# Second MoE of a fused FFT and MoE kernel: order of the products in its sums, and place of the next tile's x

## The chip, the cores and the metric

The kernel runs on one core of one Trainium2 chip. A time is the device time of one execution in microseconds (us); the figure for the kernel before is the median of three runs. Beside it stands one profiled execution, whose records the rows below come from. Its span is the time from its first to its last instruction.

## The reference

A real array x (8 x 3072 x 256) goes through two Fourier transforms, of which the real part is kept; the 24576 rows of 256 go through a first MoE layer (256 to 2048 and back), and then each row goes to one of eight experts:

```python
X = np.fft.fft(np.fft.fft(x, axis=1), axis=2).real
h = x @ w_in;  x = (h * np.clip(h + 3, 0, 6) / 6) @ w_out       # first MoE
logits = x @ w_gate                                            # second MoE, x is 24576 x 256
expert_idx = np.argmax(logits, axis=1)
gate_w = softmax(logits)[arange, expert_idx]
for e in range(8):
    xe = x[expert_idx == e]
    out[expert_idx == e] = gate_w * (np.maximum(xe @ w1[e], 0) @ w2[e])   # 256 -> 1024 -> 256
```

## The kernel before

The first 2085 us are the transforms and the first MoE, whose rows are scattered into one list per expert in HBM (`xs_dram`). The change is in what follows, the second MoE. It works through the lists in tiles of 512 rows (big) or 256 rows (small), each tile of one expert. Tiles 0 and 1 are big and belong to the fullest expert; then two or three big tiles and a small one take turns. 59 tiles run: 41 big and 18 small; the small ones are tiles 4, 7, 10, 13, 16, 20, 23 and so on up to tile 58, the last. Three more small tiles stand behind a condition at the end.

Numbers are kept as sums of two parts, a high one (rounded to the format of TensorE's products) and a low one (what the rounding left). A product of two numbers is three products of parts: high by high, high by low and low by high. For one tile (`tile_of`, L1106) this is done:

- `first` (L993), the w1 phase: eight groups of 128 inner columns, f = 0 to 7. Each group is a sum of six products (two halves k of the 256 input columns by the three of PASS, L259) into one bank of PSUM, `hp`; there are four such banks. ACT evicts the high part with the relu (L999, into `WA`), DVE makes the low part from the bank and the high part (L1000, into `WB`), and only then is the bank free.
- `second` (L1092), the w2 phase: for each 128 rows of the tile (four groups in a big tile, two in a small one) a sum of 24 products, f = 0 to 7 by the three of PASS, into a bank `op`. DVE scales it by the gate (L1100, `yo`) and POOL scatters the rows to the output (L149).
- `prep_w` (L875) splits the next tile's weights, which SP has loaded, into parts, in four pieces, two of w1 and two of w2. ACT rounds the high part (L882), and the low part is a subtraction (L189) on POOL, or on DVE for the first piece that is prepared in a small tile. There are two sets of weights: `TB`, `W2a` and `SC` with the raw loads `w1a`, `w2a`, `w2d`, and `W1b`, `W2b` with `w1b`, `w2b`; tiles take them in turn.
- `prep_x` (L887) does the same for the next tile's x. The transposing loads bring 16-bit halves; ACT copies one (L894) and DVE the other (L895) into `xf`; ACT rounds the high part (L896, `xT0`), DVE subtracts for the low part (L189, `xT1`); a cast (L900) or two small instructions (L903, L904) make the rows' addresses `dst`. There are two sets here too: `xa`, `xfa`, `xTa` and `xb`, `xfb`, `xTb`.

The code is written tile by tile (w1 of tile i, preparation for i + 1, loads for i + 2, w2 of tile i), but a scheduler sets the order in which each engine gets its instructions: it moves a preparation ahead as far as its buffers allow. On each engine the instructions then run in that order, each one waiting for what it needs. A preparation of weights stands in ACT's queue as soon as the old ones have their last reader, around the last w1 group of a tile.

Of the kernel before, what the change touches and what calls it, by code (L numbers as in the profile page):

```python
# [22 lines left out]
P = 128  # L23
NB, SEQ, D, DFF, NE, FF = 8, 3072, 256, 2048, 8, 1024
# [5 lines left out]
TBIG, TS = 512, 256  # L30
# [4 lines left out]
NEARLY = 2  # L35
# [39 lines left out]
def tile_fft_moe(ctx, tc, xr, xf, xcoef, w_in, w_out, w_gate, w1, w2, tabs, fm, misc, tri, sgn8, dstc, maskc, out):  # L75
# [70 lines left out]
    dve, act, pool, pe, sp = nc.vector, nc.scalar, nc.gpsimd, nc.tensor, nc.sync  # L146

    def scat(group, **kw):
        i = pool.indirect_dma_start(oob_is_err=False, **kw)  # L149
        tc.declare_no_dep(i.ins, group=group, reason="distinct rows")  # L150
        tc.add_to_no_dep_group(group, i.ins)
# [11 lines left out]
    def matmul(*a, **kw):  # L163
        i = pe.matmul(*a, **kw)  # L164
        if hold.get("steps"):
            tc.keep_in_program_order(i)

    def mm_group(dst, terms):
        for n, (l, r) in enumerate(terms):
            matmul(dst, l, r, start=(n == 0), stop=(n == len(terms) - 1))  # L170

    def pinned(i):
        if hold.get("fold"):
            tc.keep_in_program_order(i)
# [13 lines left out]
    def sub(eng, o, a, b):  # L188
        i = eng.tensor_tensor(out=o, in0=a, in1=b, op=ALU.subtract)  # L189
        pinned(i)  # L190
        return i
# [67 lines left out]
    PASS = ((0, 0), (0, 1), (1, 0))  # L259
# [354 lines left out]
    if True:  # L614
# [215 lines left out]
        hh = [[W.rearrange("p (f n) -> p f n", n=TBIG) for W in Ws] for Ws in (WA, WB)]  # L830
# [9 lines left out]
        def rows(i):  # L840
            return TBIG if order[i] < NBIG else TS

        def xset(i):
            return xsets[i if i < NEARLY else 2 * (i % 2)]

        def kset(i):
            return ksets[0 if i < NEARLY else (i - NEARLY + 1) % 2]
# [4 lines left out]
        def load_x(i):  # L852
            t = T[i] = {}
            n = rows(i)
            o = order[i] - NEARLY
            v = er[0:1, i:i + 1] if i < NEARLY else regs[0:1, 0, o:o + 1]
            r = ds(reg(v, NE * CAPR - n), n)
            t["gd"] = pk.tile([P, 4, 2], F32, tag="gd", name=f"gd{i}")[:, 0:n // P]
            sp.dma_start(t["gd"], xs.bitcast(F32)[r, D:D + 2].rearrange("(t p) c -> p t c", p=P))
            for w in range(2):  # L860
                for k in range(2):
                    c = w * D + k * P
                    sp.dma_start(xset(i)["x"][:, w, k, 0:n], xs16[r, c:c + P], transpose=True)

        def load_w(i):
            s = kset(i)
            o = order[i] - NEARLY
            e = reg(er[0:1, 2:3] if i < NEARLY else regs[0:1, 1, o:o + 1], NE - 1)
            sp.dma_start(s["w1"], w1[ds(e, 1)].rearrange("e (k p) f -> p (e k) f", p=P))
            for f0, f1, t in s["w2"]:  # L870
                sp.dma_start(t.rearrange("p (f d) -> p f d", d=D),
                             w2[ds(e, 1), f0 * P:f1 * P].rearrange("e (k p) d -> p (e k) d", p=P))


        def prep_w(i, eng):  # L875
            s = kset(i)
            pairs = [[t[:, k] for t in s["W1"]] + [s["w1"][:, k]] for k in range(2)]
            pairs += [[t[:, f0:f1] for t in s["W2"]] + [t.rearrange("p (f d) -> p f d", d=D)]
                      for f0, f1, t in s["w2"]]

            def go(n, hi, lo, raw):
                pinned(act.activation(hi, raw, AF.Copy))  # L882
                sub(eng(n), lo, raw, hi)

            return [lambda n=n, p=p: go(n, *p) for n, p in enumerate(pairs)]

        def prep_x(i):  # L887
            t, v = T[i], xset(i)
            n = rows(i)
            nt = n // P  # L890
            xf, t["xT"] = v["xf"][:, :, 0:n], [z[:, :, 0:n] for z in v["xT"]]
            h = xf.bitcast(U16).rearrange("p k (n w) -> p k n w", w=2)
            keep = tc.keep_in_program_order
            keep(act.activation(h[:, :, :, 1], v["x"][:, 0, :, 0:n], AF.Copy))  # L894
            keep(dve.tensor_copy(h[:, :, :, 0], v["x"][:, 1, :, 0:n]))  # L895
            act.activation(t["xT"][0], xf, AF.Copy)  # L896
            sub(dve, t["xT"][1], xf, t["xT"][0])
            t["dst"] = pk.tile([P, 4], I32, tag="dst", name=f"dst{i}")[:, 0:nt]
            if order[i] < NBIG:
                keep(dve.tensor_copy(t["dst"], t["gd"][:, :, 1]))  # L900
            else:
                inv = pk.tile([P, 2], F32, tag="inv", name=f"inv{i}")
                keep(dve.tensor_scalar(inv, iot, vld[:, order[i] - NBIG:order[i] - NBIG + 1], BIG, op0=ALU.is_lt, op1=ALU.mult))  # L903
                keep(dve.tensor_tensor(out=t["dst"], in0=inv, in1=t["gd"][:, :, 1], op=ALU.add))  # L904
# [20 lines left out]
        def plan_early():  # L925
            e0 = 8 * (NCH - EC) + 18 + RKW - 3
            fill[e0].append(lambda: None)
            pfill[e0].append(early_mm)
            fill[e0].append(early_pick)
            fill[e0 + 4].append(lambda: (first_sets(), load_x(0), load_w(0), load_x(1)))  # L930
            for n in range(4):
                fill[e0 + 6 + EG * n].append(lambda n=n: in_order(prep_w(0, lambda n: dve)[n]))
            fill[e0 + 10 + EX].append(lambda: prep_x(0))
# [59 lines left out]
        def first(i, then=None):  # L993
            s, xT, n = kset(i), T[i]["xT"], rows(i)
            for f in range(8):
                hi, lo = (h[f // 4][:, f % 4, 0:n] for h in hh)
                ps = h_ps.tile([P, 512], F32, tag="hp", name=f"hp{i}_{f}")[:, 0:n]
                mm_group(ps, [(s["W1"][a][:, k, f * P:(f + 1) * P], xT[c][:, k]) for k in range(2) for a, c in PASS])
                act.activation(hi, ps, AF.Relu)  # L999
                dve.scalar_tensor_tensor(out=lo, in0=ps, scalar=0.0, in1=hi, op0=ALU.max, op1=ALU.subtract)  # L1000
                if f == FL and then:
                    then()

        def rest():
# [5 lines left out]
            assert not (fill or pfill or mfill or afill)  # L1010

        first(0, rest)
        second_set()
        prep_x(1)


# [36 lines left out]
        def pick(r, v, o, sh):  # L1053
# [35 lines left out]
                          W1=[pt(f"W1b{n}", [P, 2, FF]) for n in range(2)], W2=[pt(f"W2b{n}", [P, 8, D]) for n in range(2)]))  # L1089
        xsets.append(dict(x=pt("xb", [P, 2, 2, TBIG], U16), xf=pt("xfb", [P, 2, TBIG], F32), xT=[pt(f"xTb{n}", [P, 2, TBIG]) for n in range(2)]))  # L1090

        def second(i):  # L1092
            s, t = kset(i), T.pop(i)
            nt = rows(i) // P
            yo = pd.tile([P, 4, D], F32, tag="yo", bufs=2, name=f"yo{i}")
            for j in range(nt):
                ps = o_ps.tile([P, 512], F32, tag="op", name=f"op{i}_{j}")
                mm_group(ps[:, 0:D], [(hh[a][f // 4][:, f % 4, j * P:(j + 1) * P], s["W2"][c][:, f]) for f in range(8)
                                      for a, c in PASS])
                dve.tensor_scalar(yo[:, j], ps[:, 0:D], t["gd"][:, j, 0:1], None, op0=ALU.mult)  # L1100
                scat("out", out=out, out_offset=IndirectOffsetOnAxis(ap=t["dst"][:, j:j + 1], axis=0),
                     in_=yo[:, j], in_offset=None, bounds_check=NTOK - 1)
# [3 lines left out]
        def tile_of(i):  # L1106
            if i:
                first(i)
            if i + 1 < last and i:
                if i + 1 >= NEARLY:  # L1110
                    for f in prep_w(i + 1, lambda n: pool if n or rows(i) == TBIG else dve):
                        f()
                prep_x(i + 1)
            if i and i + 2 < last:
                load_x(i + 2)
                load_w(i + 2)
            second(i)
# [5 lines left out]
        for i in range(last):  # L1123
            tile_of(i)
        n = nc.values_load(nus[0:1, 0:1], min_val=0, max_val=NSMALL, skip_runtime_bounds_check_because=why)
        with tc.If(n > NSMALL - SPARE):
            i0, last = last, full
            for i in range(i0, min(i0 + 2, full)):
                load_x(i)
                load_w(i)  # L1130
            for f in prep_w(i0, lambda n: pool):
                f()
            prep_x(i0)
            for i in range(i0, last):
                tile_of(i)
# [149 lines left out]
```

## Time and profile before

| | |
|---|---|
| median of the runs | 3274.42 us (3268.84 to 3277.36, three runs) |
| the profiled execution's own time | 3273.91 us |
| its span | 3272.1 us |
| mean granted clock of TensorE | 0.985 |
| second MoE: first product, tile 0 | 2088 us after the span's start |
| second MoE: last product, tile 58 | 3260 us |

The span is shared out by engines: TensorE's products (PE), its weight loads (PEld), VectorE (DVE), ScalarE (ACT), GpSimd (POOL) and SyncE's DMA queue (SP). A product is issued while the one before it is still running, so starts tell more than durations. The idle time that a row names is the time just before an instruction, with the instruction that ended it.

### The profile page before, as it was taken

What the parts mean: (1) busy time and instruction counts of PE and PEld (TensorE: products, weight loads), DVE (VectorE), ACT (ScalarE), POOL (GpSimd) and SP (SyncE); (2) the same over time, 40 slices, a digit from 0 to 9 for tenths busy, and PEclk for the clock granted to TensorE, in tenths of its full rate; (3) what the DMA queues carried; (4) which work ended last, traced back from release to release, by engine and by line L of the source; (5) the groups of instructions that cost most, each with busy time, mean ns of one, the idle gap of its engine ahead of it and who ended that gap; (6) DMA issues with size and microseconds to landing.
All of it is one profiled execution on the core that took longest, in us unless ns stands there. A gap on an engine that the chain in (4) does not pass through costs nothing.

```text
span 3272.1 us, 61901 instructions
## 1 busy us (share of the span) xinstructions
PE 3116.5 (95%) x23482; PEld 2983.7 (91%) x23482; DVE 2117.7 (65%) x3699; ACT 1952.4 (60%) x3339; POOL 2123.1 (65%) x1784
## 2 busy tenths in 40 slices
PE   5899999999999999999999999999999999999998
PEld 5889999999999999999999999988888888888887
DVE  8586777777777777777777666755555555555553
ACT  3566666666666666667666766654444454444453
POOL 5466766766766766766766665676666566666664
PEclk8899999999999999999999999999999999999999
DMA  5100100100100100100100002274555455555550
GB/s 184 62 27 16 44 24 16 43 24 16 44 24 16 44 24 16 44 24 16 34 14 16 15 14 53 63 200 149 147 154 152 140 166 152 149 147 155 145 173 26
DMA packets 256189, 243.14 MB, mean 74 GB/s; under 512 B 157739, under 2 KB 219020, under 8 KB 255888
## 3 DMA queue, kind: packets, MB, share of 16 engines
q1 hardware_dynamic: 234640, 184.66, 20.0%
q0 software_dynamic: 21248, 54.48, 4.6%
q8 instruction: 187, 3.06, 0.4%
q14 instruction: 114, 0.93, 0.1%
HBM read 159.71 MB, written 54.04 MB: 65 GB/s over the span
## 4 chain that ended last, share of the span: by engine, by line
PE 61%; DVE 22%; ACT 10%; issue 3%; POOL 2%; DMA 1%; SPq 0%; ACTq 0%; DVEq 0%; POOLq 0%
PE op L164 16%; PE acc L164 16%; PE hp L164 15%; PE ab L164 11%; DVE r L515 6%; ACT r L508 5%; DVE ab L186 3%; DVE ab L189 3%; ACT xp L546 1%; ACT gh L962 1%; DVE H L194 1%; ACT xo L539 1%; PE wi L164 1%; DVE H L186 1%; DVE xTa L189 1%
## 5 line engine op out<-in xcount | busy, mean ns | idle before, releaser
L189 POOL TENSOR_TENSOR gl<-r,gh 128x512 fp32r<-128x512 f32 x768 | 1018.7, 1349 | 541.4 <-ACT gh L962 536.7
L164 PE MATMUL acc<-WO,gh 128*128 128x264 f32 x6144 | 831.7, 286 | 4.5 <-ACT xo L539 2.3
L515 DVE SCALAR_TENSOR_TENSOR r<-r,ab 128x512 f32<-128x512 f32 x768 | 493.0, 683 | 460.8 <-ACT r L508 452.9
L164 PEld LDWEIGHTS acc<-WO,gh 128*128 128x128 f32 x6144 | 780.9, 190 | 6.5 <-ACT WO L182 3.3
L508 ACT ACTIVATE r<-ab,half 128x512 f32<-128x512 f32 x768 | 486.2, 684 | 241.0 <-DVE ab L186 219.5
L962 ACT ACTIVATE gh<-r 128x512 fp32r<-128x512 f32 x768 | 454.5, 628 | 203.2 <-PE acc L164 145.6
L1000 DVE SCALAR_TENSOR_TENSOR WB<-hp,WA 128x512 fp32r<-128x512 f32 (+1 forms) x472 | 278.7, 607 | 299.4 <-ACT WA L999 293.8
L164 PE MATMUL ab<-pq,WA 128*128 128x256 f32 x2304 | 398.3, 289 | 69.4 <-DVE r L515 63.6
L164 PE MATMUL acc<-WO,gl 128*128 128x264 f32 x3072 | 439.9, 285 | 0.0
L164 PEld LDWEIGHTS ab<-pq,WA 128*128 128x128 f32 x2304 | 330.6, 192 | 90.0 <-issue 82.4
L164 PEld LDWEIGHTS acc<-WO,gl 128*128 128x128 f32 x3072 | 402.8, 189 | 0.0
L999 ACT ACTIVATE WA<-hp 128x512 fp32r<-128x512 f32 (+1 forms) x472 | 241.4, 531 | 194.8 <-PE hp L164 192.7
L164 PE MATMUL ab<-pq,WB 128*128 128x256 f32 x2304 | 342.3, 285 | 0.0
L502 ACT ACTIVATE A<-ab 128x512 f32<-128x512 f32 x384 | 230.1, 599 | 158.7 <-PE ab L164 138.6
L149 POOL DMA_INDIRECT out_dram<-yo,dst x200 | 217.6, 1088 | 156.5 <-DVE yo L1100 119.4
L164 PEld LDWEIGHTS ab<-pq,WB 128*128 128x128 f32 x2304 | 307.7, 193 | 0.0
L164 PE MATMUL hp<-xTb,TB 128*128 128x512 f32 (+1 forms) x1344 | 277.3, 364 | 13.7 <-DVE WB L1000 13.5
L189 DVE TENSOR_TENSOR ab<-A,ab 128x512 f32<-128x512 f32 x384 | 264.7, 689 | 32.8 <-ACT A L502 25.3
L164 PEld LDWEIGHTS hp<-xTb,TB 128*128 128x128 f32 x1344 | 225.8, 188 | 57.9 <-DVE WB L1000 15.2
L164 PE MATMUL hp<-xTa,W1b 128*128 128x512 f32 (+1 forms) x1392 | 275.6, 357 | 1.6 <-DVE WB L1000 1.6
L164 PE MATMUL op<-W2b,WA 128*128 128x256 f32 x1536 | 275.0, 281 | 0.0
L186 DVE TENSOR_TENSOR ab<-A,ab 128x512 f32<-128x512 f32 x384 | 266.8, 695 | 11.5
(269 smaller groups left out, 5300.8 us busy)
## 6 DMA issues: line engine op xcount, KB each, us to landing
w1a<-in_w_dram SPq DMA_DIRECT2D x29, 1024.0 KB
w1b<-in_w_dram SPq DMA_DIRECT2D x29, 1024.0 KB
w2b<-in_w_dram SPq DMA_DIRECT2D x58, 512.0 KB
R<-in_xr_dram SPq DMA_DIRECT2D x32, 774.0 KB
w2a<-in_w_dram SPq DMA_DIRECT2D x29, 768.0 KB
w2d<-in_w_dram SPq DMA_DIRECT2D x28, 256.0 KB
q<-pq SPq DMA_DIRECT2D x288, 1.0 KB
raw<-in_w_in_dram SPq DMA_DIRECT2D x8, 512.0 KB
```

The lines of the kernel that those rows point to most:

```text
L149: i = pool.indirect_dma_start(oob_is_err=False, **kw)
L164: i = pe.matmul(*a, **kw)
L186: pinned(eng.tensor_tensor(out=o, in0=a, in1=b, op=ALU.add))
L189: i = eng.tensor_tensor(out=o, in0=a, in1=b, op=ALU.subtract)
L194: pinned(dve.scalar_tensor_tensor(out=o, in0=a, scalar=s, in1=b, op0=ALU.mult, op1=ALU.add))
L502: act.activation(A, h[0], AF.Copy)
L508: act.activation(r, h, AF.Relu, bias=half, scale=1.0 / 6.0)
L515: dve.scalar_tensor_tensor(out=g, in0=r, scalar=1.0, in1=h, op0=ALU.min, op1=ALU.mult)
L539: act.activation(xo[:, t, :], acc[t][:, 0:GW], AF.Copy)
L962: act.activation(gh[n], r[n], AF.Copy)
L999: act.activation(hi, ps, AF.Relu)
L1000: dve.scalar_tensor_tensor(out=lo, in0=ps, scalar=0.0, in1=hi, op0=ALU.max, op1=ALU.subtract)
```

## The change

Three things. In the w1 sums all products with the high part of x come first and those with its low part last. In the w2 sums all products with the high parts of the inner rows come first, f = 0 to 7, and those with the low parts last. `prep_x` of the next tile is called between the two w1 pieces and the two w2 pieces of `prep_w` instead of behind all four, and its subtraction is done in two halves.

```diff
--- before.py
+++ after.py
@@ -894,7 +894,8 @@
             keep(act.activation(h[:, :, :, 1], v["x"][:, 0, :, 0:n], AF.Copy))
             keep(dve.tensor_copy(h[:, :, :, 0], v["x"][:, 1, :, 0:n]))
             act.activation(t["xT"][0], xf, AF.Copy)
-            sub(dve, t["xT"][1], xf, t["xT"][0])
+            for k in range(2):
+                sub(dve, t["xT"][1][:, k], xf[:, k], t["xT"][0][:, k])
             t["dst"] = pk.tile([P, 4], I32, tag="dst", name=f"dst{i}")[:, 0:nt]
             if order[i] < NBIG:
                 keep(dve.tensor_copy(t["dst"], t["gd"][:, :, 1]))
@@ -995,7 +996,7 @@
             for f in range(8):
                 hi, lo = (h[f // 4][:, f % 4, 0:n] for h in hh)
                 ps = h_ps.tile([P, 512], F32, tag="hp", name=f"hp{i}_{f}")[:, 0:n]
-                mm_group(ps, [(s["W1"][a][:, k, f * P:(f + 1) * P], xT[c][:, k]) for k in range(2) for a, c in PASS])
+                mm_group(ps, [(s["W1"][a][:, k, f * P:(f + 1) * P], xT[c][:, k]) for c in range(2) for k in range(2) for a in range(2 - c)])
                 act.activation(hi, ps, AF.Relu)
                 dve.scalar_tensor_tensor(out=lo, in0=ps, scalar=0.0, in1=hi, op0=ALU.max, op1=ALU.subtract)
                 if f == FL and then:
@@ -1095,8 +1096,8 @@
             yo = pd.tile([P, 4, D], F32, tag="yo", bufs=2, name=f"yo{i}")
             for j in range(nt):
                 ps = o_ps.tile([P, 512], F32, tag="op", name=f"op{i}_{j}")
-                mm_group(ps[:, 0:D], [(hh[a][f // 4][:, f % 4, j * P:(j + 1) * P], s["W2"][c][:, f]) for f in range(8)
-                                      for a, c in PASS])
+                mm_group(ps[:, 0:D], [(hh[a][f // 4][:, f % 4, j * P:(j + 1) * P], s["W2"][c][:, f])
+                                      for a in range(2) for f in range(8) for c in range(2 - a)])
                 dve.tensor_scalar(yo[:, j], ps[:, 0:D], t["gd"][:, j, 0:1], None, op0=ALU.mult)
                 scat("out", out=out, out_offset=IndirectOffsetOnAxis(ap=t["dst"][:, j:j + 1], axis=0),
                      in_=yo[:, j], in_offset=None, bounds_check=NTOK - 1)
@@ -1107,10 +1108,9 @@
             if i:
                 first(i)
             if i + 1 < last and i:
-                if i + 1 >= NEARLY:
-                    for f in prep_w(i + 1, lambda n: pool if n or rows(i) == TBIG else dve):
-                        f()
-                prep_x(i + 1)
+                w = prep_w(i + 1, lambda n: pool if n or rows(i) == TBIG else dve) if i + 1 >= NEARLY else []
+                for f in w[:2] + [lambda: prep_x(i + 1)] + w[2:]:
+                    f()
             if i and i + 2 < last:
                 load_x(i + 2)
                 load_w(i + 2)
```

What this makes of the order is shown at three places. In these rows WA is the high and WB the low part of the inner rows (0 for f = 0 to 3, 1 for f = 4 to 7), xT0 and xT1 are the high and low part of x, W2a and SC those of w2; the names carry the tile and the group (hp7_6 is group 6 of tile 7) and a buffer number.

The first place is TensorE in small tile 7, at the end of its w1 phase. Before:

```order
L164 MATMUL op7_0_29120<-W2a0_26224,WA0_69 128x256
L164 MATMUL op7_0_29120<-SC1_74,WA0_69 128x256
L164 MATMUL op7_0_29120<-W2a0_26224,WB0_71 128x256
L164 MATMUL op7_0_29120<-W2a0_26224,WA0_69 128x256
L164 MATMUL hp7_7_29081<-xTb0_27630,TB_73 128x256
L164 MATMUL hp7_7_29081<-xTb1_27631,TB_73 128x256
L164 MATMUL hp7_7_29081<-xTb0_27630,TB_73 128x256 x2
L164 MATMUL hp7_7_29081<-xTb1_27631,TB_73 128x256
L164 MATMUL hp7_7_29081<-xTb0_27630,TB_73 128x256
L164 MATMUL op7_0_29120<-SC1_74,WA0_69 128x256
```

In the changed kernel, the same place and the end of the first w2 group:

```order
L164 MATMUL hp7_7_29089<-xTb0_27632,TB_73 128x256 x4
L164 MATMUL hp7_7_29089<-xTb1_27633,TB_73 128x256 x2
L164 MATMUL op7_0_29129<-W2a0_26224,WA0_69 128x256
L164 MATMUL op7_0_29129<-SC1_74,WA0_69 128x256
...
L164 MATMUL op7_0_29129<-W2a0_26224,WA1_70 128x256
L164 MATMUL op7_0_29129<-SC1_74,WA1_70 128x256
L164 MATMUL op7_0_29129<-W2a0_26224,WB0_71 128x256 x4
L164 MATMUL op7_0_29129<-W2a0_26224,WB1_72 128x256 x4
L164 MATMUL op7_1_29158<-W2a0_26224,WA0_69 128x256
```

Four products of the w2 group no longer stand ahead of the last w1 group, the two products with xT1 are the last of the six, and WB is asked for only after 16 products with WA.

The second place is DVE around small tile 4, whose next tile is 5. Before:

```order
L1000 SCALAR_TENSOR_TENSOR WB0_71<-hp4_3_28447,WA0_69 128x256
L189 TENSOR_TENSOR xTb1_27631<-xfb_27629,xTb0_27630 128x1024
L1000 SCALAR_TENSOR_TENSOR WB1_72<-hp4_4_28456,WA1_70 128x256
L1000 SCALAR_TENSOR_TENSOR WB1_72<-hp4_5_28465,WA1_70 128x256
L1000 SCALAR_TENSOR_TENSOR WB1_72<-hp4_6_28474,WA1_70 128x256
L900 CAST dst5_28504<-gd5_28291 128x4
L1000 SCALAR_TENSOR_TENSOR WB1_72<-hp4_7_28483,WA1_70 128x256
L1100 TENSOR_SCALAR yo4_28521<-op4_0_28522,gd4_28071 128x256
```

In the changed kernel, from the w2 phase of big tile 3 to the first eviction of tile 4:

```order
L1101 TENSOR_SCALAR yo3_28308<-op3_0_28309,gd3_27856 128x256
L189 TENSOR_TENSOR xTa1_26228<-xfa_26226,xTa0_26227 128x256 x2
L904 TENSOR_SCALAR inv4_28286<-iot_59,vld_61 128x2
L189 TENSOR_TENSOR xTb1_27633<-xfb_27631,xTb0_27632 128x512
L905 TENSOR_TENSOR dst4_28285<-inv4_28286,gd4_28075 128x2
L189 TENSOR_TENSOR xTb1_27633<-xfb_27631,xTb0_27632 128x512
L1101 TENSOR_SCALAR yo3_28308<-op3_1_28338,gd3_27856 128x256
L901 CAST dst5_28506<-gd5_28296 128x4
L1101 TENSOR_SCALAR yo3_28308<-op3_2_28367,gd3_27856 128x256
L1101 TENSOR_SCALAR yo3_28308<-op3_3_28396,gd3_27856 128x256
L1001 SCALAR_TENSOR_TENSOR WB0_71<-hp4_0_28425,WA0_69 128x256
```

The subtraction for tile 5 and its cast have left the evictions of tile 4 and stand among those of the w2 groups of tile 3; the subtraction is in two halves there.

The third place is ACT from the last w1 groups of big tile 3 into small tile 4. Before:

```order
L999 ACTIVATE WA1_70<-hp3_6_28254 128x512
L882 ACTIVATE TB_73<-w1a_26223 128x1024
L999 ACTIVATE WA1_70<-hp3_7_28263 128x512
L882 ACTIVATE TB_73<-w1a_26223 128x1024
L896 ACTIVATE xTa0_26227<-xfa_26226 128x2x256
L882 ACTIVATE W2a0_26224<-w2a_26221 128x1536
L882 ACTIVATE W2a0_26224<-w2d_27622 128x512
L999 ACTIVATE WA0_69<-hp4_0_28420 128x256
L999 ACTIVATE WA0_69<-hp4_1_28429 128x256
L894 ACTIVATE xfb_27629<-xb_27628 128x1024
L999 ACTIVATE WA0_69<-hp4_2_28438 128x256
```

In the changed kernel:

```order
L1000 ACTIVATE WA1_70<-hp3_6_28258 128x512
L882 ACTIVATE TB_73<-w1a_26223 128x1024
L1000 ACTIVATE WA1_70<-hp3_7_28267 128x512
L882 ACTIVATE TB_73<-w1a_26223 128x1024
L894 ACTIVATE xfb_27631<-xb_27630 128x1024
L896 ACTIVATE xTa0_26227<-xfa_26226 128x2x256
L896 ACTIVATE xTb0_27632<-xfb_27631 128x1024
L882 ACTIVATE W2a0_26224<-w2a_26221 128x1536
L1000 ACTIVATE WA0_69<-hp4_0_28425 128x256
L882 ACTIVATE W2a0_26224<-w2d_27624 128x512
L1000 ACTIVATE WA0_69<-hp4_1_28434 128x256
```

Copy and rounding of xb for tile 5 have moved from between the evictions of tile 4 to ahead of the w2 pieces. The rounding of TB ahead of the eviction of hp3_7 stands where it stood; of the six products of hp3_7 it now has to wait for the fifth, the last one that reads this half of TB, and before for the second. L1000 in the changed kernel is L999 before.

## Rows read from the trace of the kernel before

**Rows 1.** Busy time by engine, second MoE: PE, PEld, DVE, ACT, POOL, clock, DMA.
```profile
2085.00:3262.00 1177.00, 1145.32 (x7664) 1047.53 (x7662) 616.88 (x944) 568.68 (x823) 752.60 (x425) 1.00 0.51 146
```

**Rows 2.** Waits of weight loads, 2085 to 3262: us in total, times, longest.
```profile
PEld op L164 <- DVE WB L1000: 18.1, 18, 1.1
PEld hp L164 <- DVE WB L1000: 17.8, 10, 2.0
```

**Rows 3.** Chain that ended last, small tile 16: start, us, what.
```profile
2423.53 2.11 DVE xTb L189
...
2426.41 1.08 DVE WB L1000 x3
2427.49 1.26 DVE dst L900
2428.75 0.34 DVE WB L1000
```

**Rows 4.** Weight loads in time, tiles 2, 16, 23: start, us, what, idle before.
```profile
2141.45 1.01 PEld L164 LDWEIGHTS hp<-xTa,W1b 128*128 128x128 f32 x5 [2.01 <-DVE WB L1000]
...
2426.88 0.19 PEld L164 LDWEIGHTS op<-W2b,WB 128*128 128x128 f32 x1 [0.87 <-DVE WB L1000]
2429.13 0.19 PEld L164 LDWEIGHTS op<-W2b,WB 128*128 128x128 f32 x1 [1.12 <-DVE WB L1000]
...
2565.90 0.77 PEld L164 LDWEIGHTS hp<-xTb,TB 128*128 128x128 f32 x6 [1.90 <-DVE WB L1000]
```

**Rows 5.** Chain that ended last, w2 phase of small tiles 13 and 23.
```profile
2366.98 6.73 PE op L164 x44
...
2566.88 5.20 PE op L164 x44
```

**Rows 6.** Windows after two long waits, columns as in rows 1.
```profile
2248.20:2251.50 3.30, 3.30 (x17) 3.30 (x17) 0.45 (x2) 1.88 (x3) 2.57 (x2) 0.50 0.51 130
...
2367.70:2370.90 3.20, 3.20 (x17) 3.20 (x16) 0.59 (x2) 1.17 (x2) 3.17 (x2) 0.50 0.36 58
```

**Rows 7.** ACT in time, big tile 15 into small tile 16, columns as in rows 4.
```profile
2406.72 1.05 ACT L882 ACTIVATE TB<-w1a 128x1024 fp32r<-128x1024 f32 x1
2407.67 0.59 ACT L999 ACTIVATE WA<-hp 128x512 fp32r<-128x512 f32 x1
2408.15 1.06 ACT L882 ACTIVATE TB<-w1a 128x1024 fp32r<-128x1024 f32 x1
...
2418.23 1.49 ACT L882 ACTIVATE W2a<-w2a 128x1536 fp32r<-128x1536 f32 x1 [5.49 <-PE op L164]
```

**Rows 8.** DVE in time, w2 phase of big tile 15, columns as in rows 4.
```profile
2407.80 1.23 DVE L189 TENSOR_TENSOR TB<-w1a,TB 128x1024 fp32r<-128x1024 f32 x1 [0.25 <-ACT TB L882]
2408.95 0.68 DVE L1000 SCALAR_TENSOR_TENSOR WB<-hp,WA 128x512 fp32r<-128x512 f32 x1
...
2416.06 0.49 DVE L1100 TENSOR_SCALAR yo<-op,gd 128x256 f32<-128x256 f32 x1 [1.73 <-PE op L164]
2418.89 0.48 DVE L1100 TENSOR_SCALAR yo<-op,gd 128x256 f32<-128x256 f32 x1 [2.34 <-PE op L164]
```

**Rows 9.** TensorE's products in time, big tile 15, w1 into w2.
```profile
2404.33 3.20 PE L164 MATMUL hp<-xTb,TB 128*128 128x512 f32 x13
2407.37 0.28 PE L164 MATMUL op<-W2a,WA 128*128 128x256 f32 x1
```

**Rows 10.** Groups by line, 2030 to 3272: count, busy us, mean ns, idle before.
```profile
L189 DVE TENSOR_TENSOR xTb<-xfb,xTb 128x1024 fp32r<-128x1024 f32 x20 | 49.8, 2491 | 13.6 <-ACT xTb L896 13.6
...
L189 DVE TENSOR_TENSOR xTa<-xfa,xTa 128x1024 fp32r<-128x1024 f32 x20 | 46.2, 2309 | 12.9 <-ACT xTa L896 12.9
...
L189 DVE TENSOR_TENSOR xTe<-xfa,xTe 128x1024 fp32r<-128x1024 f32 x1 | 1.2, 1219 | 0.0
```

**Rows 11.** ACT in time, start of big tile 2, columns as in rows 4.
```profile
2136.91 1.49 ACT L882 ACTIVATE W2a<-w2a 128x1536 fp32r<-128x1536 f32 x1 [0.74 <-DMA w2a<-in_w_dram]
...
2138.89 1.35 ACT L894 ACTIVATE xfb<-xb 128x1024 uint16<-128x1024 uint16 x1
```

## The prediction

> **What bounds the kernel now.** I read four views, in this order. First the busy time of the engines in the second MoE alone (2085 to 3262 us): TensorE is busy for 1145 of 1177 us, at a granted clock of 1.00 by the mean, DVE for 617, ACT for 569 and POOL for 753 [rows 1]. So only what makes TensorE wait in this stage has a price. Second, the list of waits of TensorE's weight loads in this stage: two lines make up nearly all of it, 18.1 us in 18 waits of the w2 products and 17.8 us in 10 waits of the w1 products, all for the DVE instruction that makes the low part of the inner rows (L1000) [rows 2]. That is 35.9 us, and it is the whole of what can be won here by a better order. Third, the chain of waits around one such place, to see what held DVE back. In small tile 16 the chain leaves TensorE for ACT, then for 2.11 us of DVE on the low part of the next tile's x, then three queued L1000, then 1.26 us of a four-element cast, then the last L1000 [rows 3]. Fourth, the weight loads in order of time, where one sees how long TensorE stood: 0.87 and 1.12 us in tile 16, 1.90 us at once in tile 23 [rows 4]. The two kinds alternate: where the next tile's x goes into the b buffers, the wait falls into the w2 products (two waits, nine tiles); where it goes into the a buffers, the last w1 group of the small tile waits for its bank (one wait, eight tiles). 9 x 2 = 18, and 8 of the 10 are these, at 1.90 us as in tile 23 (15.2 us); the ninth is tile 2 with 2.01 us [rows 4], and 0.6 us are left for the tenth, in tile 0. No big tile with a big tile behind it waits. What ends last at each of the 17 places is thus DVE's work on the next x, which stands in DVE's queue between the L1000 of a small tile (5.7 us of w1 products), while in a big tile it stands behind all eight.
>
> Two further losses hang on the waits. After two of the eight long ones the granted clock is 0.50 (1.2 instead of 2.4 GHz) for some 3.4 us [rows 6]. The 44 w2 products behind the second of these waits take 6.73 us, where they take 5.20 us in tile 23 [rows 5]: 1.53 us each, 3.1 us in both.
>
> **The change, part by part.** (a) prep_x moves ahead of the two w2 pieces of prep_w. In the order of the instructions the x behind a small tile is then prepared one tile earlier, in the w2 phase of the big tile before it: on DVE the two subtractions and the cast stand among that tile's four evictions, and nothing but L1000 is left between the L1000 of the small tile. This takes away all 17 places: 18.1 us, and of the 17.8 us all but tile 2 and tile 0, so 15.2 us; together 33.3 us. Where does the moved work go? In the big tile before a small one (tile 15) DVE idles for 1.73 and 2.34 us in the w2 phase, waiting for TensorE [rows 8]. What comes in are the subtraction and the cast; the low copy of that x stood there already. A subtraction of this size took 1.22 us alone and 2.31 to 2.49 us in the mean beside POOL [rows 10], and the cast up to 1.26 us [rows 3], so 1.2 to 3.8 us into 4.1 us of room. It is hidden. If the cover were gone, the first L1000 of the small tile would be late and its fifth w1 group would wait for a bank. ACT gets the high half of the x and its rounding in the same place; there it stood idle for 5.49 us ahead of the w2 piece, waiting for TensorE [rows 7]. SP: the transposes of x are released earlier by as much as the buffers, and no DVE or ACT work on x waits for a landing in the rows read, so none is late; where the w1 and w2 loads stand behind them in SP's queue now, they are wanted only a tile later.
>
> (b) The order of products in w1. TensorE does as many. But the ACT conversion of the next w1 half overwrites the half that the last w1 group still reads. Until now its last reader was the second of six products, now it is the fifth, and this conversion stands in ACT's queue ahead of the last eviction of the tile. This is the cost of the change. In tile 15 the conversion starts at 2406.72 [rows 7]. The 13 w1 products from 2404.33 on take 0.234 us each up to the first w2 product at 2407.37, and one lasts 0.40 us [rows 9], so the fifth ends at about 2407.30 and the conversion would start at 2407.35, 0.63 us later; the last eviction then ends at 2408.89 instead of 2408.26. (c) The order in w2 asks for that eviction earlier: its high part is the 15th product of the group, no longer the 22nd. At 0.118 us a product (5.20 us by 44 [rows 5]) its weights are loaded at 2407.37 + 13 x 0.118 = 2408.90. With 0.04 us from an end to the load behind it [rows 3, 4] (2429.09 to 2429.13) the rows come at 2408.93: some 0.05 us late, in each of 38 big tiles: 1.9 us. The bounds are 0 (it can't gain) and 0.2 us a tile, if the conversion is released by the next product's end: 7.6 us. I take 1.9. In small tiles eviction and products are shorter and it fits.
>
> In the big tile before a small one DVE has a subtraction of w1 (1.23 us) ahead of its last L1000 [rows 8]. It too is 0.63 us later: L1000 ends at 2410.26 instead of 2409.63. The product that needs it is the last of the group; with one product of the next group put ahead of it, its load stands at 2407.37 + 23 x 0.118 = 2410.08, 0.22 us too early, 0.17 us once the first wait is taken off. 17 tiles: 2.9 us, between 0 and 6.8 (0.4 us). What (c) gives back: for the other tiles the low parts are now wanted from the 17th product on, 1.9 us after the w2 phase begins, while L1000 of the last group ends at about 2.3 us and is wanted at 2.6: no price. The w2 pieces are released 0.5 us later at the end of the phase (their last reader is the 22nd product, not the 18th); ACT then has no x ahead of the next tile's evictions, which pays for it.
>
> (d) The low part of x in two halves: 41 more instructions on DVE, some 0.15 us each, off the path: nothing. (e) Tile 2: its first eviction stood behind 1.35 us of x on ACT, which ran after the w2 pieces [rows 11]; now it stands ahead of them, in ACT's 0.74 us of idle time. 0.65 us of the 2.01 go. (f) The clock: without the waits I let both slow stretches go, 3.1 us; at worst none goes.
>
> **Sum.** 33.3 + 0.65 + 3.1 - 1.9 - 2.9 = 32.2 us off the span of 3272.1, so 3239.9; the profiled execution took 3273.9, 1.8 us more than its span, and gives 3241.7. That execution is 0.5 us from the median of the runs (3274.4), so I forecast 3242 us for the runs as well.
>
> **The rivals.** R1, DVE doesn't finish in the big tile. For: beside a POOL subtraction the same DVE instruction took 2.96 us at its longest in the rows read for it, and the cast 1.26. Against: POOL has one subtraction early in this phase and then only scatters. If both halves are held up, 3.8 to 5 us go into 4.1 minus the 0.6 that (b) takes; up to 1.0 us is late in front of a small tile, 17 us in 17 tiles: 3242 + 17 = 3259.
> The Trainium skill, SBUF — State Buffer, section "SBUF: two separate sides", says that a DVE instruction with two SBUF inputs and a GpSimd instruction take a shared pair of ports in turn, each for its whole length, and this speaks against the change, since two halves can be held up twice. By that rule R1 would be the forecast if POOL ran subtractions there; the trace agrees with the price (1.22 us alone against 2.49 in the mean) but not with the place.
>
> R2, the boundary waits of (b) and (c) come at their upper ends: 7.6 + 6.8 = 14.4 us instead of 4.8, and the clock keeps its two slow stretches: 3242 + 9.6 + 3.1 = 3255.
>
> R3, the other side: slower. The same conversion, ahead of ACT's last eviction in all 55 tiles that prepare weights, holds w2 up by more than 37.0 / 55 = 0.67 us a tile, for instance if ACT's and DVE's work behind it is delayed as a whole and the next tile's banks are late as well. At 1 us a tile that is 3274 - 37 + 55 = 3292. Against it: the eviction can't start earlier than its own last product allows, and this is one product after the conversion's.
>
> R4, no change: DVE was not the bound, and another producer (POOL's low halves of w2, now behind all scatters of a tile) ends just as late. 3274. Against it: POOL idles for a third of the stage [rows 1], and no weight load waits for POOL now [rows 2].
>
> **Chances.** Forecast 0.76, R1 0.09, R2 0.08, R4 0.04, R3 0.03. What a measurement of this kernel can tell from no change is about 0.3%, 10 us. Faster: forecast, R1 and R2, 0.93, of which 0.01 goes to the middle for an R1 that comes out larger: 0.92; within 0.3%, R4 and this: 0.05; slower: 0.03. The range goes from 3231 (all 39.0 us gone and the runs 4 us low, as the shown ones differ) to 3256, which takes in R2 and the smaller half of R1.
>
> **What would show it.** Right: the two lines of weight loads waiting for L1000 shrink from 28 waits to a few of tenths of a us; no DVE instruction on x in the chain of waits; in small tiles the w1 phase takes 5.7 us and w2 5.6. For (b): the conversion ahead of the last eviction starts at about the first w2 product, and weight loads of the w2 products wait a little for ACT's eviction (L999 here, one line lower in the changed code). Wrong: waits of 0.5 us or more ahead of the fifth w1 group of small tiles (R1), waits for ACT of 0.2 us or more in every big tile (R2, R3), or waits for POOL (R4).

## The result and the profile after

| | before | changed |
|---|---|---|
| median of the runs | 3274.42 us (3268.84 to 3281.15, five runs) | 3237.3 us (3234.43 to 3238.52, five runs) |
| ratio, 95% interval | 1 | 0.9892 [0.9879, 0.9904] |
| profiled execution, its span | 3273.91, 3272.1 us | 3238.52, 3236.7 us |
| mean granted clock | 0.985 | 0.986 |
| first w1 product of the fourth tile to the last w2 product | 1101.2 us | 1065.4 us |

The changed kernel is faster by 37.1 us (1.1%). The forecast was 3242 us, the range 3231 to 3256. The last line of the table, taken from the start times of the products in the trace, is what I compare below under the name *stage*. In the traces of this study the second MoE starts between 2081 and 2094 us and its first three tiles take 68.6 to 70.6 us; inside the stage, big tiles in which nothing waits take the same 22.5 or 22.6 us in the kernel before and in kernels 1, 5 and 6 below.

The first view is the second MoE in one window, which answers to [rows 1] (columns as there):

```profile
2085.00:3227.00 1142.00, 1138.74 (x7672) 1047.42 (x7671) 589.33 (x1002) 584.14 (x823) 730.70 (x425) 1.00 0.54 151
```

TensorE is without work for 3 us of this window, where it was 32 us before. The waits of its weight loads, which answer to [rows 2]:

```profile
PEld hp L164 <- DVE WB L1001: 1.8, 2, 1.2
```

Of 28 waits and 35.9 us, two are left, in tiles 0 and 2 (L1001 is L1000 of before, L1000 is L999). From the first product of a small tile to the first of the next tile it takes 11.27 us (tile 16) and 11.45 us (tile 23), where it took 13.48 and 13.46. The half-clock stretches of [rows 6] are gone too; the windows around the same two tiles, columns as in [rows 1]:

```profile
2245.00:2252.00 7.00, 7.00 (x52) 6.58 (x51) 1.39 (x3) 4.96 (x7) 6.36 (x5) 1.00 0.71 176
2365.00:2371.00 6.00, 6.00 (x28) 4.85 (x27) 2.77 (x4) 3.13 (x6) 5.76 (x3) 1.00 0.68 228
```

What came in shows in big tile 15, where the w2 products begin at 2396.91. First ACT in order of time, which answers to [rows 7]:

```profile
2396.93 1.06 ACT L882 ACTIVATE TB<-w1a 128x1024 fp32r<-128x1024 f32 x1 [0.55 <-PE hp L164]
2397.89 0.58 ACT L1000 ACTIVATE WA<-hp 128x512 fp32r<-128x512 f32 x1
2398.37 1.05 ACT L882 ACTIVATE TB<-w1a 128x1024 fp32r<-128x1024 f32 x1
...
2402.95 1.06 ACT L896 ACTIVATE xTb<-xfb 128x1024 fp32r<-128x1024 f32 x1
2408.58 1.49 ACT L882 ACTIVATE W2a<-w2a 128x1536 fp32r<-128x1536 f32 x1 [4.57 <-PE op L164]
```

The conversion of w1 now starts with the first w2 product, not 0.65 us ahead of it, and waits for TensorE to let go of its half. The last eviction stands behind it and ends at 2398.47, 1.56 us after the first w2 product. Then DVE, which answers to [rows 8]:

```profile
2398.02 1.23 DVE L189 TENSOR_TENSOR TB<-w1a,TB 128x1024 fp32r<-128x1024 f32 x1 [0.92 <-ACT TB L882]
2399.16 0.68 DVE L1001 SCALAR_TENSOR_TENSOR WB<-hp,WA 128x512 fp32r<-128x512 f32 x1
2399.76 2.45 DVE L895 COPY xfa<-xa 128x512 uint16<-128x512 uint16 x1
2402.11 0.75 DVE L895 COPY xfb<-xb 128x1024 uint16<-128x1024 uint16 x1
...
2404.04 0.69 DVE L189 TENSOR_TENSOR xTb<-xfb,xTb 128x512 fp32r<-128x512 f32 x1
...
2404.72 0.68 DVE L189 TENSOR_TENSOR xTb<-xfb,xTb 128x512 fp32r<-128x512 f32 x1
...
2405.72 0.16 DVE L901 CAST dst<-gd 128x4 int32<-128x4 f32 x1
2405.92 0.48 DVE L1101 TENSOR_SCALAR yo<-op,gd 128x256 f32<-128x256 f32 x1
2408.78 0.48 DVE L1101 TENSOR_SCALAR yo<-op,gd 128x256 f32<-128x256 f32 x1 [2.38 <-PE op L164]
```

The low part of small tile 17's x (xTb) and its cast cost 1.5 us here, and behind them DVE still idles for 2.38 us, waiting for TensorE. The last L1001 ends at 2399.84, 2.93 us after the first w2 product. What both cost TensorE stands in its products, which answer to [rows 9]:

```profile
2398.45 0.28 PE L164 MATMUL op<-SC,WA 128*128 128x256 f32 x1
2398.57 0.34 PE L164 MATMUL op<-W2a,WA 128*128 128x256 f32 x1
2398.75 0.28 PE L164 MATMUL op<-SC,WA 128*128 128x256 f32 x1
...
2399.70 0.28 PE L164 MATMUL op<-W2a,WA 128*128 128x256 f32 x1
2399.90 0.39 PE L164 MATMUL op<-W2a,WB 128*128 128x256 f32 x1
2400.12 0.28 PE L164 MATMUL op<-SC,WA 128*128 128x256 f32 x1
```

Starts are 0.12 us apart, save at two places: 0.18 us at the 15th product (the late high part) and 0.20 and 0.22 us around the one that reads the last low part. The list of waits does not show either.

### The profile page after: what moved, and what is told of

The parts are those of the page before. It is cut to its first block, busy times and chain, and to the rows that moved or that the text cites. A ratio compares the mean times of both kernels' runs of the same rounds, so it can differ in the third digit from the quotient of the medians.

```text
span 3236.7 us, 61919 instructions
## 1 busy us (share of the span) xinstructions
PE 3109.2 (96%) x23482; PEld 2982.6 (92%) x23482; DVE 2093.6 (65%) x3758; ACT 1966.9 (61%) x3339; POOL 2097.9 (65%) x1784
## 5 line engine op out<-in xcount | busy, mean ns | idle before, releaser
L1001 DVE SCALAR_TENSOR_TENSOR WB<-hp,WA 128x512 fp32r<-128x512 f32 (+1 forms) x472 | 284.8, 609 | 327.3 <-ACT WA L1000 326.3
L1000 ACT ACTIVATE WA<-hp 128x512 fp32r<-128x512 f32 (+1 forms) x472 | 246.9, 528 | 228.7 <-PE hp L164 226.6
L149 POOL DMA_INDIRECT out_dram<-yo,dst x200 | 206.2, 1031 | 177.9 <-DVE yo L1101 124.6
L164 PEld LDWEIGHTS hp<-xTa,W1b 128*128 128x128 f32 x1392 | 226.9, 188 | 39.6 <-DVE WB L1001 1.2
```

## The experiments

Ten kernels were run, each a few lines from one of the two. *Stage* is as above, taken from one profiled execution.

| kernel | median | ratio to before, 95% interval | stage |
|---|---|---|---|
| changed | 3237.3 | 0.9892 [0.9879, 0.9904] | 1065.4 |
| 1 only the moved x | 3235.8 | 0.9886 [0.9871, 0.9902] | 1061.8 |
| 2 only the w2 order | 3247.2 | 0.9920 [0.9907, 0.9934] | 1076.4 |
| 3 changed, w1 order of before | 3236.3 | 0.9892 [0.9876, 0.9907] | 1064.4 |
| 4 changed, w2 order of before | 3232.6 | 0.9874 [0.9856, 0.9892] | 1060.9 |
| 5 before, queue places one further back | 3243.5 | 0.9918 [0.9905, 0.9932] | 1069.2 |
| 6 before, x behind all evictions | 3232.8 | 0.9880 [0.9865, 0.9895] | 1063.3 |
| 7 as 4, w1 subtraction behind the last L1000 | 3227.3 | 0.9863 [0.9848, 0.9878] | 1055.8 |
| 8 only the w1 order | 3271.0 | 0.9998 [0.9989, 1.0007] | 1099.5 |
| 9 changed, x subtracted whole | 3232.6 | 0.9885 [0.9867, 0.9902] | 1065.8 |
| 10 changed, w1 subtraction as in 7 | 3236.0 | 0.9891 [0.9871, 0.9910] | 1063.2 |

Medians of different groups of runs differ by a few us in the kernel before as well (3270.7 to 3274.4), so small differences are read from the stage.

**1. Only the moved x.** From the kernel before:

```
-                if i + 1 >= NEARLY:
-                    for f in prep_w(...): f()
-                prep_x(i + 1)
+                w = prep_w(...) if i + 1 >= NEARLY else []
+                for f in w[:2] + [lambda: prep_x(i + 1)] + w[2:]: f()
```

> Only the move of the next tile's x (between w1 and w2 pieces); both product orders and the undivided subtraction as before. Theory M (the move alone removes the waits, the product orders only cost): the 28 waits of the weight loads for L1000 shrink to one or two, small tiles take 5.7 + 5.6 us, and the two product orders being gone their price goes too (2.9 us of late low parts): 3237 - 3 = 3234 us, 3232 to 3238. Rival O (the order of the w2 products is what removes the waits of the w2 products): 18.1 us stay, about 3255 us.

Measured: 3235.8 us, and in the list of waits

```profile
PEld hp L164 <- DVE WB L1000: 1.8, 2, 1.4
```

The stage is 39.5 us shorter than before, 3.6 us more than in the changed kernel. So the move alone takes away all of the waits, and the two product orders together cost something, as theory M had it. The intervals of the whole runs overlap; the stage tells them apart.

**2. Only the w2 order.** From the kernel before:

```
-    mm_group(..., [... for f in range(8) for a, c in PASS])
+    mm_group(..., [... for a in range(2) for f in range(8) for c in range(2 - a)])
```

> Only the order of the w2 products (low parts of the inner rows last). Theory M: the last low part is wanted at the 23rd product instead of the 24th and comes as late as before, so the 18.1 us of waits stay in the w2 products (two per tile become one of about 2 us), and the 17.8 us in the w1 products stay: 3274 us, 3270 to 3278. Rival O: the waits of the w2 products go, those of the w1 products stay: 3274 - 18 = 3256 us, or less.

Here theory M failed: 3247.2 us, and

```profile
PEld hp L164 <- DVE WB L1000: 1.3, 3, 0.5
```

Even the waits of the w1 products went, which no order of w2 products can reach by itself. DVE in small tile 16 of this kernel, columns as in [rows 4]:

```profile
2415.22 2.22 DVE L189 TENSOR_TENSOR xTb<-xfb,xTb 128x1024 fp32r<-128x1024 f32 x1 [0.47 <-ACT xTb L896]
2417.36 1.07 DVE L1000 SCALAR_TENSOR_TENSOR WB<-hp,WA 128x256 fp32r<-128x256 f32 x3
2418.36 1.36 DVE L900 CAST dst<-gd 128x4 int32<-128x4 f32 x1
```

Against [rows 3], the cast of 1.3 us is now behind the last L1000 and not ahead of it. Not all of the loss is gone: the small tiles take 11.9 and 12.3 us here, where kernel 1 takes 11.4 and 11.3, some 12 us in all 17. They stand in waits of 0.1 to 0.2 us at single products, too short for the list. In tile 16 the eight products with the low parts take longer in the first w2 group, while the three L1000 behind the subtraction end, than in the second:

```profile
2417.35 1.52 PE L164 MATMUL op<-W2b,WB 128*128 128x256 f32 x8
...
2420.59 1.10 PE L164 MATMUL op<-W2b,WB 128*128 128x256 f32 x8
```

So the low parts are late in this kernel too, as theory M had it, but by far less. The order of DVE's instructions in the two kernels (no times; - before, + this one) in small tiles 4 and 7 shows the new places in both kinds of tile:

```
 L1000 SCALAR_TENSOR_TENSOR WB_71<-hp_3_28447,WA_69 128x256
+L1000 SCALAR_TENSOR_TENSOR WB_72<-hp_4_28456,WA_70 128x256
 L189 TENSOR_TENSOR xTb_27631<-xfb,xTb_27630 128x1024
-L1000 SCALAR_TENSOR_TENSOR WB_72<-hp_4_28456,WA_70 128x256
...
+L1000 SCALAR_TENSOR_TENSOR WB_72<-hp_7_28483,WA_70 128x256
 L900 CAST dst_28504<-gd_28291 128x4
-L1000 SCALAR_TENSOR_TENSOR WB_72<-hp_7_28483,WA_70 128x256

+L1000 SCALAR_TENSOR_TENSOR WB_71<-hp_3_29045,WA_69 128x256
 L189 TENSOR_TENSOR xTa_26228<-xfa,xTa_26227 128x1024
-L1000 SCALAR_TENSOR_TENSOR WB_71<-hp_3_29045,WA_69 128x256
```

The scheduler places DVE's instructions by what it expects of TensorE, and another order of products has moved the x work and the cast by one place each. In the second kind of tile the last w1 group takes the bank of hp_3; its L1000 no longer stands behind the subtraction. In the eight tiles of this kind TensorE's own queue has changed as well: the last w1 group no longer stands behind four w2 products. From all this came a new theory, P: the places in the queue made the 26 us, not the order of the products.

**3 and 4. The changed kernel without one of its orders.** The edits put back the line of before in `first` (3) or in `second` (4).

> The changed kernel with the w1 products in their order of before. The W1 conversion starts some 0.7 us ahead of the end of the w1 products again, the last inner row's low part in the big tile before a small one ends at 2.3 instead of 2.93 us after it. Theory L (late low parts cost 0.2 us in 17 tiles): the w2 phases of those tiles fall from 11.66 to 11.45 us: 3.3 us less. What the w1 phases do tells whether the w1 order itself is worth something: 11.11 to 11.17 us in the big tiles of the changed kernel against 11.19 to 11.24 before. If the order makes that (theory W), they go back to 11.2, 0.07 x 41 = 2.9 us more, and the sum is 3237 us; if not (rival: something else, such as the clock or the moved x), they stay and the time is 3234 us.

> The changed kernel with the w2 products in their order of before. The waits of the small tiles stay away under theory M (the move of x removes them): 3237 us, 3233 to 3239; the last low part is wanted one product later (0.12 us), so the late low parts of the 17 big tiles before small ones cost 0.1 instead of 0.2 us each (1.7 us less), and if the w2 order itself is what lengthens the w2 phases without such a wait from 11.36 to 11.42 us, they fall back, 0.06 x 41 = 2.5 us less: 3233 us. Rival O: 18 us of waits come back in the w2 products: 3255 us.

3: the w2 phases of the 17 tiles ahead of small ones went from 11.55 to 11.68 us down to 11.39 to 11.42, and the big tiles' w1 phases from 11.11 to 11.23 or 11.26 us in tiles with an even number and from 11.17 to 11.20 in the others: theories L and W both hold, and they nearly cancel (the stage is 0.9 us shorter). 4: the waits stay away, the w2 phases without a late low part fall from 11.41 to 11.26 and from 11.43 to 11.32 us (medians of even and odd tiles). The late low part, though, costs more in the old order (0.26 to 0.38 us of a phase, not the 0.1 I expected), and the list of waits now shows it:

```profile
PEld op L164 <- DVE WB L1001: 3.5, 17, 0.2
```

**5 and 6. The places alone.** Both are the kernel before, its orders of products and its place of prep_x in the code; three instructions are put behind an eviction by hand (k is 4 or 3 in the first, 7 in the second):

```
-            act.activation(t["xT"][0], xf, AF.Copy)
-            sub(dve, t["xT"][1], xf, t["xT"][0])
+            with tc.issue_after(hold["ev", k]) if small else nul():
+                act.activation(t["xT"][0], xf, AF.Copy)
+            with tc.issue_after(hold["lo", k]) if small else nul():
+                sub(dve, t["xT"][1], xf, t["xT"][0])
...
+                with tc.issue_after(hold["lo", 7]) if small else nul():
                     keep(dve.tensor_copy(t["dst"], t["gd"][:, :, 1]))
```

> The kernel before with both product orders as before and x prepared in the same place of the code; alone the queue places of three instructions in small tiles are set by hand: the low part of the next x (and the ACT rounding it needs) goes one L1000 further back, behind the fifth (b buffers) or the fourth (a buffers), and the four-element cast goes behind the last L1000. These are the places on DVE that the run with the w2 order alone had. Theory P (that run won 26 us because the w2 order made the scheduler move these instructions by one place, not by the order of the products): most of the 26 us come here too, and without the 0.1 us that the w2 order costs in each big tile: 3246 us, 3241 to 3252. Rival O (the order of the products is what needs the low parts later): the waits stay, 3266 to 3274 us.

> As the run before, but the low part of x and the cast stand behind all eight L1000 of the small tile, in its own w2 phase. Theory P: no L1000 of the small tile waits, so the 28 waits go as with the moved x; what is late next is the x itself: the rounding on ACT stands behind the last eviction and ends about 2.2 to 3.3 us after the w1 products, the subtraction takes 2.2 to 3 us, so the next tile's low x is there 4.4 to 6.3 us after the w1 products, where its first w1 product comes after 5.6 us and the first that needs a low part 0.2 us later: between nothing and 0.5 us a tile, 3236 to 3245 us, I take 3239. Rival (x in a small tile is late anyway, the room is only in the big tile): 1 us or more in 17 tiles, 3252 us or more.

The waits in 5, then in 6 (L1006 is L1000 of before):

```profile
PEld op L164 <- DVE WB L1006: 4.8, 9, 0.5
PEld hp L164 <- DVE WB L1006: 2.8, 3, 2.0
```

```profile
PEld hp L164 <- DVE WB L1006: 2.4, 3, 1.7
```

In kernel 5 no x work moved to another tile. In the nine small tiles whose next x goes into the b buffers TensorE's queue is that of before, and one place in the queues of DVE and ACT takes them from 13.50 to 11.95 us. In the eight others (13.45 to 11.58 us) the last w1 group again no longer stands behind four w2 products. It waits for a bank that L1000 frees, whichever place it has, but no kernel moved it alone. Together this is worth 32.0 us of the stage, 3.1 of them the two slow stretches; theory P holds and rival O falls. The nine waits of 0.5 us that 5 keeps are the L1000 still queued behind the subtraction. In 6 they are gone as well, and the x is nearly in time within the small tile: the nine tiles take 11.36 us, as in kernel 1, the eight 11.50 in place of 11.34. I had put this at 3239 us, 3236 to 3245; it came out at 3232.8. DVE there, with the x and the cast last:

```profile
2420.47 2.33 DVE L189 TENSOR_TENSOR xTb<-xfb,xTb 128x1024 fp32r<-128x1024 f32 x1 [0.52 <-ACT xTb L900]
2422.72 2.38 DVE L906 CAST dst<-gd 128x4 int32<-128x4 f32 x1
```

**8. Only the w1 order.** From the kernel before, the new line in `first`.

> Only the order of the w1 products (low x last). The x work keeps its places on DVE in the small tiles, so theory M and P both leave the 28 waits of 35.9 us and add the late low parts in 17 big tiles (0.26 us each, 4.4 us), less 0.1 us in each second big tile for the order itself: 3274 + 4.4 - 2.5 = 3276 us, 3271 to 3280. Rival (the low x being last gives the next tile's x time and takes the waits of the w1 products): 3258 us.

The time is that of before. The waits (3.6 us more in the w2 products, 17 of them the late low part) are all there:

```profile
PEld op L164 <- DVE WB L1000: 21.7, 35, 1.1
PEld hp L164 <- DVE WB L1000: 18.6, 12, 2.6
```

**7 and 10. The late low part.** The DVE subtraction of a w1 half goes behind the last L1000 of the big tile; 7 starts from kernel 4, 10 from the changed one:

```
+                with tc.issue_after(hold["lo", i - 2]) if eng(n) is dve and i > 3 and rows(i - 2) == TBIG else ExitStack():
                     sub(eng(n), lo, raw, hi)
```

> The changed kernel with the w2 products in their order of before and the DVE subtraction of a w1 half queued behind the last L1000 of the big tile, not ahead of it (17 tiles). Theory L (this subtraction is what makes the last low part late, 0.23 to 0.28 us in 17 tiles): the w2 phases of these tiles fall from 11.58 and 11.64 us to 11.32 and 11.26, the 17 waits of 3.5 us in all go: from 3232.6 to 3228 us, from the fourth tile to the end 1056.5 instead of 1060.9 us. Rival: the subtraction then holds up the x work or the w2 evictions behind it, and the time is the same or more (3233 to 3236).

> The changed kernel, both its product orders kept, with the DVE subtraction of a w1 half queued behind the last L1001 of the big tile in 17 tiles. Theory L (this subtraction makes the last low part late, 0.2 us in 17 tiles): from the fourth tile to the end 1065.4 - 3.4 = 1062.0 us, the median 3234 us; the intervals behind the 24th w2 product of these tiles lose 0.17 to 0.2 us, the 0.04 to 0.08 us at the 15th (the late high part) stay. Rival: the late high part is what costs there: 1065 us, no change.

7 is the fastest kernel of this study, 0.9863 [0.9848, 0.9878] of before. Its stage is 5.1 us shorter than that of 4, and all the w2 phases fell to 11.26 and 11.32 us. DVE at the same place (L1002 is L1001 of the changed kernel, L896 its L895):

```profile
2395.11 0.69 DVE L1002 SCALAR_TENSOR_TENSOR WB<-hp,WA 128x512 fp32r<-128x512 f32 x1 [1.40 <-ACT WA L1001]
2395.72 0.46 DVE L896 COPY xfa<-xa 128x512 uint16<-128x512 uint16 x1
2396.06 1.21 DVE L189 TENSOR_TENSOR TB<-w1a,TB 128x1024 fp32r<-128x1024 f32 x1
```

In 10 the stage is 2.2 us shorter, not the 3.4 I expected; the intervals around the 24th w2 product are gone, those at the 15th (0.04 to 0.08 us) are not.

**9. The halves.** The changed kernel with the one subtraction of before in `prep_x`.

> The changed kernel with the low part of x subtracted in one piece again (where the two halves were apart in DVE's queue, with an eviction of w2 between them, it now stands ahead of that eviction). Theory (the halves cost and give nothing, being off the path): 3237 us, 3234 to 3240, from the fourth tile to the end 1065.4 us within 0.5. Rival (the halves let a w2 eviction through and so spare the banks a wait, or their fixed time costs): more than 1 us to either side.

The stage is 1065.8 against 1065.4 us: the halves neither cost nor give anything that can be seen. The median, 3232.6 us, is below the 3234 that I had as the least, in a group of runs in which the kernel before has the lowest median too (3270.7).

## Why the prediction was right, step by step

**(a) The waits.** The mechanism is shown: the 28 waits go with the moved x alone (kernel 1), and some of them are there, long or short, as long as x work or the cast stands ahead of an L1000 of the small tile (2, 5, 6 and 8 against each other). Its size was too small. Without the slow stretches of (f), the 17 small tiles got 36.5 us shorter in kernel 1 (in the mean nine by 2.16, eight by 2.13 us), and I had 33.3 us from the list of waits. The list counts until the weight load starts; the product behind the one that waited then starts 0.22 to 0.23 us after it and not 0.12, as in tile 16 of the kernel before:

```profile
2426.88 0.39 PE L164 MATMUL op<-W2b,WB 128*128 128x256 f32 x1 [0.66 <-DVE WB L1000]
2427.11 0.40 PE L164 MATMUL op<-W2b,WA 128*128 128x256 f32 x2
2427.34 0.28 PE L164 MATMUL op<-W2b,WB 128*128 128x256 f32 x1
...
2429.13 0.38 PE L164 MATMUL op<-W2b,WB 128*128 128x256 f32 x1 [0.92 <-DVE WB L1000]
2429.35 0.40 PE L164 MATMUL op<-W2b,WA 128*128 128x256 f32 x2
```

By the starts of its products this tile loses 2.12 us, where the list has 0.87 and 1.12. The eight tiles of the other kind lose 0.15 us more at the first two products of the sixth w1 group (in tile 23 at 2562.05 and 2562.27 us), too short for the list. In all, this is 3.2 us.

What I did not see is that the moved x was not needed for most of this: I took (c) as a cost, and the w2 order alone is worth 25 us, because it moved instructions in the queues (kernel 5). In the changed kernel both act on the same waits and are not added. I had looked at where the change puts x, not at what each part of it does to the queues alone.

**(b) and (c), the late high part.** The conversion starts at the first w2 product (I had 0.02 us ahead of it), the eviction ends at 1.56 us (I had 1.52). The 15th product is 0.03 to 0.08 us late in 28 of 38 tiles, about 1.5 us in all, against 1.9 forecast. That the two are so near is partly luck: by the forecast's own figures (2408.93 after 2408.90) it was 0.03 us a tile and not 0.05, or 1.1 us in all. **The late low part:** L1001 ends at 2.93 us (I had 2.89), its product is 0.17 to 0.20 us late in 17 tiles, 3.3 us against 2.9. Both in the bounds. Kernel 10 gives 2.2 us back when only this is taken away; where the other 1.1 us went stays open.

**The orders themselves** were not in the sum. Without any late part the w2 order makes the stage 2.7 us longer (kernel 3 against 1), and the w1 order makes the w1 phases 3.6 us shorter in sum (kernel 3 against the changed one). The two nearly cancel by chance; what is left of my error is mainly the 3.2 us of (a).

**(d)** Nothing, as kernel 9 shows, though the halves are 59 more instructions and not 41 (118 subtractions of x where there were 59). **(e)** Tile 2's wait fell from 2.01 to 1.23 us, by 0.78 where I had 0.65. Tiles 0 to 2 together take 0.5 us less (70.3 to 69.8), which is inside what they vary by from trace to trace. **(f)** Both slow stretches went, 3.1 us. That they follow from long waits is only half shown: kernel 8 has the same long waits, and one stretch, in tile 51, where the kernel before has two, in tiles 7 and 13. So this term is about 1.6 us (the w2 phase takes 9.9 us in place of 8.3) behind some of the long waits, and not behind others. None of the ten traces without these long waits has such a stretch in the stage; why only some of the waits bring one stays open.

**The sum.** For the stage: 36.5 and 3.1 us of (a) and (f) off, 1.5 and 3.3 on, and the two orders 2.7 on and 3.6 off: 35.7 us, measured 35.9. With 0.5 us less in tiles 0 to 2, and the first product of the second MoE 1.0 us later (2089.25 after 2088.26; the change does not touch what lies ahead of it), the span is 35.4 us shorter; the forecast was 32.2. These 3.2 us are most of the 4.7 between the forecast of 3242 us and the median; 1.2 more come from the profiled execution, which is that far above the median of its runs.

**The rivals.** R1: the price was real, the harm not. In tile 15 of the changed kernel the copy of 128x512 into xfa takes 2.45 us, where the same copy takes 0.46 us in kernel 7. Over just that time POOL subtracts:

```profile
2399.50 2.40 POOL L189 TENSOR_TENSOR TB<-w1a,TB 128x1024 fp32r<-128x1024 f32 x1 [7.04 <-ACT TB L882]
```

But 2.38 us of room were left behind it. The Trainium skill (SBUF — State Buffer, section "SBUF: two separate sides") says that GpSimd and a DVE instruction that has two SBUF inputs, or runs in a mode with two ports, shut each other out for a whole instruction. This pair agrees, if the copy runs in such a mode, which no row here shows: it ends 0.3 us after POOL's subtraction. R1's own sum was too low: 5 us into 3.5 us of room leaves 1.5 us a tile and not 1.0, so 3268 us. R2's bounds were not reached, R3 and R4 did not occur.

## What to carry to other kernels

Where a scheduler places instructions, another order on one engine can move them on the others: compare the queues of each part of a change alone before its gain is ascribed to the part that was meant. Here a long instruction for the next tile was best put behind all evictions of this one, whichever of the two tiles it stood in; one place too early cost 1.5 to 1.9 us a tile. A sum from the list of waits is a lower bound: each restart costs a little more, and short waits are not in the list, as the 12 us in kernel 2.

## What was not expected of the hardware

Products of one shape do not all take the same time. In big tiles of kernel 1 with an even number the w2 products start 118.7 ns apart in the mean, in odd ones 117.9; with the w2 order they are 118.7 and 119.0 (kernel 3). The w1 order moves the w1 products from 234.3 to 231.5 ns in even tiles (kernel 3 against the changed one), and the w2 products there from 118.7 to 117.3 ns (kernel 1 against kernel 7, both with the w2 order of before). The lists show no wait at these places. What makes the difference (which operands follow on which, or where they lie) was not tried and stays open.

A cast of four elements a partition took 2.38 us behind the subtraction in kernel 6, 1.36 us in kernel 2 (tile 16 in both) and 0.16 us in tile 15 of the changed kernel. At the first two POOL was subtracting, in kernel 6 and then in kernel 2:

```profile
2419.30 5.77 POOL L189 TENSOR_TENSOR W1b<-w1b,W1b 128x1024 fp32r<-128x1024 f32 x2
```

```profile
2416.76 5.29 POOL L189 TENSOR_TENSOR W1b<-w1b,W1b 128x1024 fp32r<-128x1024 f32 x2 [0.41 <-ACT W1b L882]
```
